# Reordering the last output tiles of a six-layer cross network and sharing them among three engines, on one Trainium2 core

## The chip, the cores and the metric

The kernel runs on one core of one Trainium2 chip. The metric is device time in microseconds (us). A profile of one execution comes with each kernel; its span, from the first to the last instruction, is about 1.7 us shorter than the device time (128.2 us for 129.92 in the profiled run of the kernel before). Runs are compared in their fast state only.

## The reference

```python
# x0: 4096 x 416, ws: 6 x 416 x 416, bs: 6 x 416, all bf16
def reference(x0, ws, bs):
    x = x0
    for l in range(ws.shape[0]):
        x = x0 * (x @ ws[l] + bs[l]) + x
    return x
```

## The kernel before

The 4096 rows are worked in four groups of 1024. The 416 features are held transposed, as three chunks of 128 ("main") and 32 left over ("tail rows"). The last layer of the last group is done differently: TensorE produces eight output tiles of 128 rows in their natural orientation in PSUM, with the sums of earlier layers added by identity matmuls, and VectorE finishes each as (PSUM + 1) * x0. Then the tiles are stored. This end is all that the change touches.

TensorE's end:

```python
nat_tile(0); nat_tile(1)            # 3 matmuls each, 128x128 by 128x416
pe.wait_ge(s_q, NC)
nat_sums(0); nat_sums(1)            # 3 identity matmuls each
nat_tile(2); nat_sums(2)
# ... waits ...
for r in range(2):                  # the tail rows of all eight tiles, in two halves
    # ... r == 1 waits for VectorE's last layer result (s_xb, s_qD) ...
    for g in range(4):              # 32-row matmuls on four row tiles, into tile t = 2g + r
        pe.matmul(ps[:, NAT_BANKS[t], 0:D], lhsT=xt_sb[...], rhs=wl_sb[...], start=t >= 3, ...)
    for g in range(4):
        ins = pe.matmul(ps[:, NAT_BANKS[t], DF:D], lhsT=xot_sb[...], rhs=ident[...], start=False, ...)
ins.then_inc(s_nt, 3)               # tiles 0, 1 and 2 are complete
for t in range(3, JS):              # JS = 8
    nat_tile(t)
    nat_sums(t).then_inc(s_nt, 1)
```

VectorE's end and the stores (two tiles each, from the queues of SyncE and ScalarE in turn):

```python
for t in range(JS):
    dve.wait_ge(s_nt, max(t + 1, 3))
    dve.scalar_tensor_tensor(out=o_sb[:, j0 + t, :], in0=ps[:, NAT_BANKS[t], 0:D], scalar=1.0,
        in1=x0n_sb[:, t, :], op0=ALU.add, op1=ALU.mult).then_inc(s_o, 1)
# SyncE:
for j in (0, 4):
    sp.wait_ge(s_o, j + 2)
    sp.dma_start(out_v[:, j0 + j:j0 + j + 2, :], o_sb[:, j0 + j:j0 + j + 2, :]).then_inc(s_out, 16)
sp.wait_ge(s_out, 16 * (NS + 3))
# ScalarE: the same for j in (2, 6)
```

Of the kernel before, what the change touches and what calls it, by code (L numbers as in the profile page):

```python
# [7 lines left out]
ALU = mybir.AluOpType  # L8
# [3 lines left out]
def bass_standalone__dcn_v2_cross__recsys_kernel(  # L12
# [20 lines left out]
    with ExitStack() as es:  # L33
# [15 lines left out]
        t32_sb = sb("t32_sb", [128, 2, G], FP32)  # L49
        x0n_sb = sb("x0n_sb", [128, JS, D])  # L50
        wl_sb = sb("wl_sb", [128, D])
        xo_sb = sb("xo_sb", [128, NS, NC, SB])
        xot_sb = sb("xot_sb", [128, NS, G])
        ot_sb = sb("ot_sb", [128, NS, 2, 128])
# [26 lines left out]
        s_x0n, s_wl, s_nt = sem("s_x0n"), sem("s_wl"), sem("s_nt")  # L81
        s_ta, s_xt, s_sw = sem("s_ta"), sem("s_xt"), sem("s_sw")
        s_oT, s_ot, s_otc = sem("s_oT"), sem("s_ot"), sem("s_otc")
        s_out, s_o = sem("s_out"), sem("s_o")

        x0_v = x0.rearrange("(j p) d -> p j d", p=128)
        out_v = out.rearrange("(j p) d -> p j d", p=128)
# [19 lines left out]
            return ps[HALVES[h], 6 + h, 0:G]  # L107

        j0 = (NS - 1) * JS

        def load_wt(eng, g, a, b, done):
            n0, n1 = ((0, 256), (256, DF))[g % 2]
# [4 lines left out]
        @block.sync  # L117
        def _(sp):
            def load_rows(s):
                sp.dma_start_transpose(  # L120
                    x4_sb[:, s - 1:s, :], x0[s * SB:(s + 1) * SB, D - 128:D]
                ).then_inc(s_x4[s - 1], 16)
                sp.dma_start_transpose(
                    x0T_sb[:, :, s * SB:(s + 1) * SB], x0[s * SB:(s + 1) * SB, 0:DF]
                ).then_inc(s_x0T[s], 16)

            sp.dma_start(bsa_sb[1:L + 1, :], bs[:, :]).then_inc(s_bs, 16)
            sp.dma_start(xin_sb[:, 0:2, :], x0_v[:, 0:2, :]).then_inc(s_xin[0], 16)
            sp.dma_start(xin_sb[:, 4:6, :], x0_v[:, 4:6, :]).then_inc(s_xin[2], 16)
            sp.dma_start_transpose(x0T_sb[:, :, 768:SB], x0[768:SB, 0:DF]).then_inc(s_x0T[0], 16)  # L130
            for l in range(1, L):
                if l > 1:
                    sp.wait_ge(s_ti, (1, 2, 2, 2)[l - 2])
                if l == L - 1:
                    load_rows(1)
                sp.dma_start(w_sb[:, l, :, :], wmain(l)).then_inc(s_w[l], 16)
                if l == 1:
                    for g in range(4):
                        load_wt(sp, g, 1, L, s_wt[1])
            for s in range(NS - 1):  # L140
                n = (s + 1) * L
                sp.wait_ge(s_xa, NC * n)
                sp.wait_ge(s_xb, NC * n)
                for c in range(NC):
                    sp.dma_start_transpose(
                        o_sb[:, s * JS:(s + 1) * JS, c * 128:(c + 1) * 128], xo_sb[:, s, c, :]
                    ).then_inc(s_oT, 16)
                sp.wait_ge(s_xt, n)
                sp.dma_start_transpose(ot_sb[:, s, :, :], xot_sb[:, s, :]).then_inc(s_ot, 16)
                if s < NS - 2:  # L150
                    load_rows(s + 2)
                if s == 0:
                    for g in range(4):
                        sp.dma_start(wl_sb[lane(g), :], ws[L - 1, DF:D, :]).then_inc(s_wl, 16)
                if s == 1:
                    sp.dma_start(x0n_sb[:, :, :], x0_v[:, (NS - 1) * JS:NS * JS, :]).then_inc(s_x0n, 16)
                sp.wait_ge(s_oT, 16 * NC * (s + 1))
                sp.wait_ge(s_otc, s + 1)
                sp.dma_start(
                    out_v[:, s * JS:(s + 1) * JS, :], o_sb[:, s * JS:(s + 1) * JS, :]  # L160
                ).then_inc(s_out, 16)
            for j in (0, 4):
                sp.wait_ge(s_o, j + 2)
                sp.dma_start(
                    out_v[:, j0 + j:j0 + j + 2, :], o_sb[:, j0 + j:j0 + j + 2, :]
                ).then_inc(s_out, 16)
            sp.wait_ge(s_out, 16 * (NS + 3))

        @block.gpsimd
        def _(pool):  # L170
            pool.memset(ones_sb[:, :], 1.0).then_inc(s_ones, 1)
            def load_wc(i, g):
                a, b = ((0, 1), (1, L))[i]
                pool.dma_start(
                    wc_sb[lane(g), a:b, 32 * g:32 * g + 32], ws[a:b, DF:D, DF:D].rearrange("l p n -> p l n")
                ).then_inc(s_wc[i], 16)

            pool.wait_ge(s_ones, 1)
            pool.affine_select(
                out=ident[:, :], in_=ones_sb[:, 0:128], pattern=[[-1, 128]],  # L180
                compare_op=ALU.is_equal, fill=0.0, base=0, channel_multiplier=1,
            ).then_inc(s_set, 1)
            pool.affine_select(
                out=u_sb[:, :], in_=ones_sb[0:L + 1, 0:L], pattern=[[1, L]],
                compare_op=ALU.is_ge, fill=0.0, base=1, channel_multiplier=-1,
            ).then_inc(s_set, 1)
            for g in (0, 2):
                load_wt(pool, g, 0, 1, s_wtp)
            pool.wait_ge(s_zero, 1)
            for i in range(2):  # L190
                for g in (1, 3):
                    load_wc(i, g)

            for s in range(NS):
                pool.wait_ge(s_te, s + 1)
                for l in range(L):
                    n = s * L + l + 1
                    if n == NL:
                        break
                    if n == 1:  # L200
                        pool.tensor_scalar(
                            out=cq_sb[:, 0:NC + 1], in0=cb_sb[:, :, L - 1], scalar1=-1.0, scalar2=None, op0=ALU.add
                        ).then_inc(s_cq, 1)
                        pool.wait_ge(s_cq, 1)
                        pool.tensor_tensor(
                            out=cq_sb[:, NC + 1:NC + 2], in0=cq_sb[:, NC:NC + 1], in1=cb_sb[:, NC, L - 2:L - 1], op=ALU.subtract
                        ).then_inc(s_cq, 1)
                    pool.wait_ge(s_ta, n)
                    dst = xot_sb[:, s, :] if l == L - 1 else xt_sb[:, (l + 1) % 2, 0:G]
                    pool.tensor_tensor(  # L210
                        out=dst, in0=t32_sb[:, n % 2, :], in1=x0t_sb[:, s, 0:G], op=ALU.mult
                    ).then_inc(s_xt, 1)
                    if n == NL - 1:
                        pool.tensor_scalar(
                            out=xot_sb[:, s, :], in0=t32_sb[:, n % 2, :], scalar1=cq_sb[:, NC + 1:NC + 2], scalar2=None, op0=ALU.add
                        ).then_inc(s_qt, 1)
                    if l == 2 and s > 0:
                        pool.wait_ge(s_ot, 16 * s)
                        pool.tensor_copy(
                            out=o_sb[:, (s - 1) * JS:s * JS, DF:D].rearrange("p (g r) f -> p r g f", r=2),  # L220
                            in_=ot_sb[:, s - 1, :, :].rearrange("p r (g f) -> p r g f", f=DR),
                        ).then_inc(s_otc, 1)

        @block.tensor
        def _(pe):
# [172 lines left out]
            def nat_tile(t):  # L398
                rows = slice(t * 128, t * 128 + 128)
                for k in range(NC):  # L400
                    if k == 0 and t < 3:
                        pe.wait_ge(s_xa, NC * (NL - 1))
                        pe.wait_ge(s_q, t + 1)
                    pe.matmul(  # L404
                        ps[:, NAT_BANKS[t], 0:D], lhsT=xT_sb[:, (L - 1) % 2, k, rows], rhs=w_sb[:, L - 1, k, :],
                        start=t < 3 and k == 0, stop=True, skip_group_check=True,
                    )

            def nat_sums(t):
# [10 lines left out]
            pe.wait_ge(s_q, NC)  # L420
            nat_sums(0)
            nat_sums(1)
            nat_tile(2)
            nat_sums(2)
            pe.wait_ge(s_xt, NL - 1)
            pe.wait_ge(s_qt, 1)
            pe.wait_ge(s_wl, 64)
            for r in range(2):
# [4 lines left out]
                for g in range(4):  # L433
                    t, rows = 2 * g + r, slice(r * 128, r * 128 + 128)
                    pe.matmul(  # L435
                        ps[:, NAT_BANKS[t], 0:D], lhsT=xt_sb[lane(g), (L - 1) % 2, rows], rhs=wl_sb[lane(g), :],
                        start=t >= 3, stop=True, skip_group_check=True, tile_position=(32 * g, 0),
                    )
                for g in range(4):
                    t, rows = 2 * g + r, slice(r * 128, r * 128 + 128)  # L440
# [1 line left out]
                        ps[:, NAT_BANKS[t], DF:D], lhsT=xot_sb[lane(g), NS - 1, rows], rhs=ident[lane(g), lane(g)],  # L442
                        start=False, stop=True, skip_group_check=True, tile_position=(32 * g, 0),
                    )
            ins.then_inc(s_nt, 3)
            for t in range(3, JS):
                nat_tile(t)
                nat_sums(t).then_inc(s_nt, 1)

        @block.vector  # L450
        def _(dve):
# [41 lines left out]
            ).then_inc(s_qD, 1)  # L493
            dve.wait_ge(s_x0n, 16)
            for t in range(JS):
                dve.wait_ge(s_nt, max(t + 1, 3))  # L496
                dve.scalar_tensor_tensor(  # L497
                    out=o_sb[:, j0 + t, :], in0=ps[:, NAT_BANKS[t], 0:D], scalar=1.0,
                    in1=x0n_sb[:, t, :], op0=ALU.add, op1=ALU.mult,
# [3 lines left out]
        def _(act):  # L503
# [26 lines left out]
            for s in range(NS):  # L530
                for l in range(L):
# [27 lines left out]
                    if l >= 3 and s < NS - 1:  # L559
# [7 lines left out]
                            )  # L567
                        if l == L - 1:
                            ins.then_inc(s_te, 1)
            for j in (2, 6):  # L570
                act.wait_ge(s_o, j + 2)
                act.dma_start(
                    out_v[:, j0 + j:j0 + j + 2, :], o_sb[:, j0 + j:j0 + j + 2, :]
                ).then_inc(s_out, 16)


# [26 lines left out]
```

## Time and profile before

| what | value | where it is read |
|---|---|---|
| time | 129.84 us, median of 3 | runs |
| span | 128.2 us | page |
| first row-tile matmul of layer one | 8.25 us | timeline, below |
| first final VectorE tile, last one's end | 121.60, 125.68 us | timeline |
| last store: issue to landing | 2.1 us | DMA issues |

In the code the first layer waits for the input loads, and its start depends on them. It is read in the timeline as the first matmul of the 32-row form (columns: start, duration, engine, line, operation, tiles and shapes):

```profile
8.25 0.37 PE L358 MATMUL ps<-x0t_sb,wt_sb 32*128 32x512 bf16 x1
```

What lies between this moment and the end of the span, 128.18 - 8.25 = 119.93 us, I call **the count**. By the page, 90% of the chain that ended last is TensorE and 6% VectorE, and the count is what the change can alter, and it separates the change from the loads.

### The profile page before, as it was taken

The page shows a single profiled execution, that of the slowest core. Times are in us where ns is not written, and L with a number is a line of the kernel's source. Part 1 is how long each engine was busy: PE and PEld are TensorE (multiplying, and loading weights), DVE is VectorE, ACT ScalarE, POOL GpSimd, SP SyncE. Part 2 cuts the span into 40 slices and gives each one's busy share as a digit, 9 for nine tenths or more (in the row PEclk, how much of TensorE's full clock was granted, in tenths as well). Part 3 has the DMA queues.
Part 4 walks back from the last instruction along what each step waited for, and adds up shares of the span by engine and source line. Part 5 has one row for each costly group of instructions (what it writes and reads, how often), then busy time and mean ns, then how long its engine had stood idle before and what let it go on. Part 6 is the DMA issues. An engine that isn't in the chain of part 4 may idle for free.

```text
span 128.2 us, 5183 instructions
## 1 busy us (share of the span) xinstructions
PE 124.0 (97%) x2338; PEld 62.3 (49%) x2338; DVE 100.7 (79%) x156; ACT 68.9 (54%) x156; POOL 22.2 (17%) x42
## 2 busy tenths in 40 slices
PE   7999999999999999999999999999999999999990
PEld 5654444445444445445445445445445445444560
DVE  2349779779779779779779789788788798797792
ACT  0637357377736456476745555575754564567500
POOL 7512202102102103012012023022022023020400
PEclk9999999999999999999999999999999999999999
DMA  3973399500009699810008699940008900700025
GB/s 98 287 187 100 81 213 204 139 5 0 5 5 158 121 113 227 248 42 5 0 5 161 115 145 232 353 134 0 5 0 91 181 5 0 250 21 5 0 98 168
DMA packets 33601, 13.48 MB, mean 105 GB/s; under 512 B 24871, under 2 KB 33581, under 8 KB 33581
## 3 DMA queue, kind: packets, MB, share of 16 engines
q1 hardware_dynamic: 31804, 12.12, 45.9%
q10 hardware_dynamic: 1584, 0.99, 2.8%
q8 instruction: 18, 0.29, 1.0%
q0 software_dynamic: 192, 0.06, 0.2%
q14 instruction: 3, 0.02, 0.1%
HBM read 3.86 MB, written 3.41 MB: 57 GB/s over the span
## 4 chain that ended last, share of the span: by engine, by line
PE 90%; DVE 6%; ACT 1%; DVEq 0%; issue 0%; ACTq 0%
PE ps L227 79%; PE ps L358 10%; DVE o_sb L497 3%; DVE xT_sb L486 3%; PE ps L277 1%; ACT xo_sb L520 1%; DVE xo_sb L491 1%; DVEq L33 0%; PE ps L435 0%; PE ps L374 0%; PE ps L441 0%; DVEq L496 0%; ACTq L537 0%
## 5 line engine op out<-in xcount | busy, mean ns | idle before, releaser
L486 DVE SCALAR_TENSOR_TENSOR xT_sb<-ps,cb_sb,x0T_sb 128x512 bf16<-128x512 f32 x120 | 81.0, 745 | 16.5 <-PE ps L358 16.5
L227 PE MATMUL ps<-xT_sb,w_sb 128*32 128x512 bf16 (+1 forms) x1596 | 84.2, 364 | 0.0
L227 PEld LDWEIGHTS ps<-xT_sb,w_sb 128*32 128x32 bf16 x1596 | 40.9, 97 | 37.2 <-issue 4.0
L516 ACT ACTIVATE xt_sb<-xt_sb 32x256 bf16<-32x256 bf16 x76 | 31.5, 414 | 15.8 <-POOL xt_sb L210 15.1
L545 ACT ACTIVATE t_sb<-ps,cb_sb 64x256 f32<-64x256 f32 x46 | 21.6, 469 | 28.7 <-PE ps L227 28.4
L210 POOL TENSOR_TENSOR xt_sb<-t_sb,x0t_sb 128x256 bf16<-128x256 f32 x20 | 13.5, 674 | 81.5 <-ACT t_sb L545 81.5
L227 PE MATMUL ps<-x0T_sb,w_sb 128*32 128x512 bf16 (+1 forms) x336 | 18.8, 369 | 0.1
L486 DVE SCALAR_TENSOR_TENSOR xo_sb<-ps,cb_sb,x0T_sb 128x512 bf16<-128x512 f32 x18 | 12.1, 743 | 2.5 <-PE ps L358 2.5
L227 PEld LDWEIGHTS ps<-x0T_sb,w_sb 128*32 128x32 bf16 x336 | 8.7, 98 | 7.9 <-issue 1.3
L358 PE MATMUL ps<-xt_sb,wt_sb 32*128 32x512 bf16 x76 | 11.5, 379 | 0.0
L564 ACT ACTIVATE x0t_sb<-x_sb 32x256 bf16<-32x256 bf16 x24 | 9.9, 413 | 0.4
L374 PE MATMUL ps<-xt_sb,wt_sb 32*128 32x512 bf16 x38 | 7.4, 385 | 0.0
L358 PE MATMUL ps<-xt_sb,wc_sb 32*128 32x256 bf16 x76 | 7.3, 268 | 0.0
L358 PEld LDWEIGHTS ps<-xt_sb,wt_sb 32*128 32x128 bf16 x76 | 2.2, 92 | 8.1 <-DVE xT_sb L486 8.1
L404 PE MATMUL ps<-w_sb,xT_sb 128*128 128x416 bf16 x24 | 5.4, 340 | 0.0
L358 PEld LDWEIGHTS ps<-xt_sb,wc_sb 32*128 32x128 bf16 x76 | 3.8, 93 | 2.2
L497 DVE SCALAR_TENSOR_TENSOR o_sb<-ps,x0n_sb 128x416 bf16<-128x416 f32 x8 | 4.1, 582 | 0.7 <-PE ps L441 0.7
L210 POOL TENSOR_TENSOR xot_sb<-t_sb,x0t_sb 128x256 bf16<-128x256 f32 x3 | 2.0, 673 | 12.6 <-ACT t_sb L545 12.6
L520 ACT ACTIVATE xo_sb<-ps,cq_sb 128x512 bf16<-128x512 f32 x5 | 3.3, 686 | 1.1 <-PE ps L358 1.1
L227 PE MATMUL ps<-const-bfloat16-1.0 128*32 128x256 bf16 x44 | 2.7, 416 | 0.8 <-PEq L588 0.8
L511 ACT ACT_TABLE_LOAD x1 | 1.3, 1283 | 3.6 <-issue 3.6
L404 PEld LDWEIGHTS ps<-w_sb,xT_sb 128*128 128x128 bf16 x24 | 2.0, 98 | 1.4 <-DVE xT_sb L486 0.4
(44 smaller groups left out, 34.4 us busy)
## 6 DMA issues: line engine op xcount, KB each, us to landing
out_dram<-o_sb SPq DMA_DIRECT2D x3, 832.0 KB, 4.9
w_sb<-in_ws_dram SPq DMA_DIRECT2D x5, 312.0 KB, 4.4
x0n_sb<-in_x_dram SPq DMA_DIRECT2D x1, 832.0 KB, 5.6
xin_sb<-in_x_dram SPq DMA_DIRECT2D x2, 208.0 KB, 3.4
out_dram<-o_sb SPq DMA_DIRECT2D x2, 208.0 KB, 2.0
out_dram<-o_sb ACTq DMA_DIRECT2D x2, 208.0 KB, 2.1
w_sb<-in_ws_dram ACTq DMA_DIRECT2D x1, 312.0 KB, 3.7
xin_sb<-in_x_dram ACTq DMA_DIRECT2D x1, 208.0 KB, 2.6
```

The lines of the kernel that those rows point to most:

```text
L210: pool.tensor_tensor(out=dst, in0=t32_sb[:, n % 2, :], in1=x0t_sb[:, s, 0:G], op=ALU.mult).then_inc(s_xt, 1)
L227: return pe.matmul(dst, lhsT=lhsT, rhs=rhs, start=start, stop=True, skip_group_check=True, tile_position=(0, 32 * q),)
L358: return pe.matmul(dst, lhsT=lhsT, rhs=srct[lane(g), cols], start=l == 0 and start, stop=True, skip_group_check=True, tile_position=(32 * ...
L374: pe.matmul(ps[:, NC * h + 2, :], lhsT=wt_sb[lane(g), l, 0:128], rhs=srct[lane(g), :].rearrange("p (b r) -> p b r", b=2)[:, ::-1, :], star ...
L404: pe.matmul(ps[:, NAT_BANKS[t], 0:D], lhsT=xT_sb[:, (L - 1) % 2, k, rows], rhs=w_sb[:, L - 1, k, :], start=t < 3 and k == 0, stop=True, sk ...
L486: dve.scalar_tensor_tensor(out=dst, in0=ps[:, NC * half + c, :], scalar=cb_sb[:, c, l:l + 1], in1=x0T_sb[:, c, o:o + H], op0=ALU.add, op1= ...
L497: dve.scalar_tensor_tensor(out=o_sb[:, j0 + t, :], in0=ps[:, NAT_BANKS[t], 0:D], scalar=1.0, in1=x0n_sb[:, t, :], op0=ALU.add, op1=ALU.mul ...
L511: act.activation(out=x0T_sb[:, 1, h * 256:(h + 1) * 256], in_=psT[:, IN_BANKS[h][1], 0:256], func=ACTF.Copy).then_inc(s_inA, 1)
L516: ins = act.activation(out=buf[lane(g), G:2 * G], in_=buf[lane(g ^ 1), 0:G], func=ACTF.Copy)
L520: act.activation(out=xo_sb[:, NS - 1, c, half * H:(half + 1) * H], in_=ps[:, NC * half + c, :], func=ACTF.Identity, bias=cq_sb[:, c:c + 1] ...
L545: ins = act.activation(out=t32_sb[HALVES[h], n % 2, :], in_=tail(h), func=ACTF.Identity, bias=cb_sb[HALVES[h], NC, l:l + 1],)
L564: ins = act.activation(out=x0t_sb[lane(g), s + 1, swap * G:(swap + 1) * G], in_=x4_sb[96:128, s, r * G:(r + 1) * G], func=ACTF.Copy,)
```

## The change

Its intent: keep TensorE from waiting for VectorE inside the tail rows, take two of eight tiles off VectorE, and make the last store half as large. The core of the diff:

```diff
+            store(sp, 0, 2, 1, 1)          # tiles 0-1 after 1 VectorE and 1 GpSimd tile
+            store(sp, 2, 4, 2, 2)
+            store(sp, 7, 8, 6, 0)
+            sp.wait_ge(s_out, 16 * (NS + 4))
 ...
+            for i, t in enumerate(POOL_TILES):      # GpSimd, POOL_TILES = (1, 3)
+                pool.wait_ge(s_oA, i + 1)
+                pool.tensor_tensor(out=o_sb[:, j0 + t, :], in0=a32_sb[:, i, :], in1=x0n_sb[:, t, :],
+                    op=ALU.mult).then_inc(s_oP, 1)
 ...
-            nat_tile(2)
-            nat_sums(2)
+            for t in (2, 3):
+                nat_tile(t)
+                nat_sums(t)
 ...
-            ins.then_inc(s_nt, 3)
-            for t in range(3, JS):
+            ins.then_inc(s_nt, 4)
+            for t in range(4, JS):
 ...
             for t in range(JS):                     # VectorE
+                if t in POOL_TILES:
+                    continue
 ...
+            for i, t in enumerate(POOL_TILES):      # ScalarE
+                act.wait_ge(s_nt, 4)
+                act.activation(out=a32_sb[:, i, :], in_=ps[:, NAT_BANKS[t], 0:D],
+                    func=ACTF.Identity, bias=1.0).then_inc(s_oA, 1)
+            store(act, 4, 6, 4, 0)
+            store(act, 6, 7, 5, 0)
```

In the built programs SyncE has 56 instructions where it had 53, GpSimd 59 for 56, ScalarE 194 for 192, VectorE 162 for 164.

More of the change, by code (lines that the diff above doesn't have):

```diff
@@ L51, in bass_standalone__dcn_v2_cross__recsys_kernel @@
         wl_sb = sb("wl_sb", [128, D])
+        a32_sb = sb("a32_sb", [128, 2, D], FP32)
         xo_sb = sb("xo_sb", [128, NS, NC, SB])
@@ L83, in bass_standalone__dcn_v2_cross__recsys_kernel @@
         s_oT, s_ot, s_otc = sem("s_oT"), sem("s_ot"), sem("s_otc")
-        s_out, s_o = sem("s_out"), sem("s_o")
+        s_out, s_o, s_oP, s_oA = sem("s_out"), sem("s_o"), sem("s_oP"), sem("s_oA")
         x0_v = x0.rearrange("(j p) d -> p j d", p=128)
@@ L109, in bass_standalone__dcn_v2_cross__recsys_kernel, with store @@
         j0 = (NS - 1) * JS
+        POOL_TILES = (1, 3)
+        def store(eng, a, b, by_dve, by_pool):
+            eng.wait_ge(s_o, by_dve)
+            if by_pool:
+                eng.wait_ge(s_oP, by_pool)
+            eng.dma_start(out_v[:, j0 + a:j0 + b, :], o_sb[:, j0 + a:j0 + b, :]).then_inc(s_out, 16)
         def load_wt(eng, g, a, b, done):
@@ L161, in _ @@
                 ).then_inc(s_out, 16)
-            for j in (0, 4):
-                sp.wait_ge(s_o, j + 2)
-                sp.dma_start(
-                    out_v[:, j0 + j:j0 + j + 2, :], o_sb[:, j0 + j:j0 + j + 2, :]
-                ).then_inc(s_out, 16)
-            sp.wait_ge(s_out, 16 * (NS + 3))
+            store(sp, 0, 2, 1, 1)
+            store(sp, 2, 4, 2, 2)
+            store(sp, 7, 8, 6, 0)
+            sp.wait_ge(s_out, 16 * (NS + 4))
         @block.gpsimd
@@ L222, in _ @@
                         ).then_inc(s_otc, 1)
+            pool.wait_ge(s_x0n, 16)
+            for i, t in enumerate(POOL_TILES):
+                pool.wait_ge(s_oA, i + 1)
+                pool.tensor_tensor(
+                    out=o_sb[:, j0 + t, :], in0=a32_sb[:, i, :], in1=x0n_sb[:, t, :], op=ALU.mult
+                ).then_inc(s_oP, 1)
         @block.tensor
@@ L403, in nat_tile @@
                         pe.wait_ge(s_q, t + 1)
+                    if k == 0 and t == 3:
+                        pe.wait_ge(s_ta, NL - 1)
                     pe.matmul(
                         ps[:, NAT_BANKS[t], 0:D], lhsT=xT_sb[:, (L - 1) % 2, k, rows], rhs=w_sb[:, L - 1, k, :],
-                        start=t < 3 and k == 0, stop=True, skip_group_check=True,
+                        start=t < 4 and k == 0, stop=True, skip_group_check=True,
                     )
@@ L436, in _ @@
                         ps[:, NAT_BANKS[t], 0:D], lhsT=xt_sb[lane(g), (L - 1) % 2, rows], rhs=wl_sb[lane(g), :],
-                        start=t >= 3, stop=True, skip_group_check=True, tile_position=(32 * g, 0),
+                        start=t >= 4, stop=True, skip_group_check=True, tile_position=(32 * g, 0),
                     )
@@ L495, in _ @@
             for t in range(JS):
-                dve.wait_ge(s_nt, max(t + 1, 3))
+                if t in POOL_TILES:
+                    continue
+                dve.wait_ge(s_nt, max(t + 1, 4))
                 dve.scalar_tensor_tensor(
@@ L569, in _ @@
                             ins.then_inc(s_te, 1)
-            for j in (2, 6):
-                act.wait_ge(s_o, j + 2)
-                act.dma_start(
-                    out_v[:, j0 + j:j0 + j + 2, :], o_sb[:, j0 + j:j0 + j + 2, :]
-                ).then_inc(s_out, 16)
+            for i, t in enumerate(POOL_TILES):
+                act.wait_ge(s_nt, 4)
+                act.activation(
+                    out=a32_sb[:, i, :], in_=ps[:, NAT_BANKS[t], 0:D], func=ACTF.Identity, bias=1.0
+                ).then_inc(s_oA, 1)
+            store(act, 4, 6, 4, 0)
+            store(act, 6, 7, 5, 0)
 _INS = ['x0', 'ws', 'bs']
```

## The prediction

> **What bounds the kernel now.** I first read the page of the kernel before (share per engine), then its chain of waits, then the timeline of the last ten microseconds, then short windows with the transfer rate. A change at the end of the program can only be read from the end. The page says 97% TensorE, and the chain agrees up to 116 us: blocks of 84 matmuls back to back, which the change doesn't touch. From there the chain leaves TensorE:
>
> ```profile
> 116.17 0.70 ACT xo_sb L520
> ...
> 116.89 3.39 DVE xT_sb L486 x5
> 120.28 0.67 DVE xo_sb L491
> 120.95 0.14 issue
> 121.08 0.35 PE ps L435 x2
> ...
> 121.60 3.58 DVE o_sb L497 x7
> ```
>
> Columns: start, duration, what. VectorE's last layer operations end at 120.95, TensorE adds the second half of the "tail rows" (L435, L441), and VectorE then finishes eight output tiles. The timeline shows how near TensorE is to it:
>
> ```profile
> 120.29 0.33 PE L412 MATMUL ps<-ident,xo_sb 128*128 128x128 bf16 x3
> 120.55 0.35 PE L435 MATMUL ps<-wl_sb,xt_sb 32*128 32x416 bf16 x4
> ...
> 121.08 0.36 PE L435 MATMUL ps<-wl_sb,xt_sb 32*128 32x416 bf16 x4 [0.16 <-DVE xo_sb L491]
> ...
> 121.60 4.08 DVE L497 SCALAR_TENSOR_TENSOR o_sb<-ps,x0n_sb 128x416 bf16<-128x416 f32 x8 [0.66 <-PE ps L441]
> ...
> 122.71 2.37 SPq L164 DMA_DIRECT2D out_dram<-o_sb  x2
> ...
> 123.72 2.40 ACTq L572 DMA_DIRECT2D out_dram<-o_sb  x2
> ...
> 124.71 0.33 PE L412 MATMUL ps<-ident,xo_sb 128*128 128x128 bf16 x3
> ```
>
> TensorE stands idle 0.16 us inside the tail matmuls, and its last matmul ends at 124.71+0.33 = 125.04. VectorE's eight tiles take 4.08 us, the first starting at 121.60; with 0.58 for the last, the pitch is (4.08-0.58)/7 = 0.50, the last runs 125.09 to 125.68. So VectorE and TensorE reach the last tile within 0.05 us of one another: **two chains are tied**. After the compute, 2.5 of the 128.2 us are left for the last store. Windows of 0.2 us there (last two columns: share of the 16 DMA engines, GB/s):
>
> ```profile
> 126.40:126.60 0.20, 0.00 (x0) 0.00 (x0) 0.00 (x0) 0.00 (x0) 0.00 (x0) 1.00 0.00 0
> 126.60:126.80 0.20, 0.00 (x0) 0.00 (x0) 0.00 (x0) 0.00 (x0) 0.00 (x0) 1.00 0.65 225
> 126.80:127.00 0.20, 0.00 (x0) 0.00 (x0) 0.00 (x0) 0.00 (x0) 0.00 (x0) 1.00 1.07 366
> 127.00:127.20 0.20, 0.00 (x0) 0.00 (x0) 0.00 (x0) 0.00 (x0) 0.00 (x0) 1.00 1.04 354
> 127.20:127.40 0.20, 0.00 (x0) 0.00 (x0) 0.00 (x0) 0.00 (x0) 0.00 (x0) 1.00 0.39 121
> 127.40:127.60 0.20, 0.00 (x0) 0.00 (x0) 0.00 (x0) 0.00 (x0) 0.00 (x0) 1.00 0.00 0
> ```
>
> The last store is issued at 125.71, its data move from about 126.66 to 127.27 (0.61 us for 208 KB, the engines full), it lands 2.1 us after issue (127.8), and the end follows 0.4 us later. So a store costs about **0.95 us before the first byte, its bytes at some 350 GB/s, 0.55 us after the last byte**. The first store is issued at 122.71; its data begin at 123.6, and between the four stores the engines rest 0.3 us or so each.
>
> [...] The trace has 597 ns (512 columns) and 377 ns (256 columns) for copies out of PSUM, a slope of 0.86[...]. [...] The final operation reads PSUM and one SBUF tile. No run so far has GpSimd beside it; GpSimd's product beside the like-formed layer operation takes a steady 0.67 us.
>
> **Part 1: tail rows one tile later.** Tile 3's six matmuls, pitch 0.70 us (starts of L404 122.09, 122.79, 123.48, 124.18), move in front of the tail. First tail half: 120.55+0.70 = 121.25. By then VectorE's last layer result (120.95) is there, so the second half follows without the 0.16 us of idle: about 0.25 us after the first, 121.50, where it was 0.53 after. TensorE then starts tile 4 at 121.81 (0.31 after the second half, as before: 121.08 to 121.39). Before, tile 4 started at 122.09. **TensorE gains 0.28 us.** Its last matmul ends at 124.76. The price: the signal that frees tiles 0 to 3 comes with the tail, and the first VectorE start moves from 121.60 to about 122.03 (121.50 plus the 0.52 from second half to VectorE, 121.08 to 121.60). **The finishing starts 0.43 later.** The new wait on ScalarE's read of the tail bank was fulfilled at 118.42; it costs nothing.
>
> **Part 2: two tiles to ScalarE and GpSimd.** VectorE loses 2 x 0.50 = 1.0 us. Its tiles are 0 (122.03), 2 (122.53), 4 (123.03), 5 (123.53), 6 and 7. A tile can start about 0.95 us after its first matmul on TensorE (0.53+0.33 to its last matmul's end, 0.1 for the signal). Tile 5 is there at 121.81+0.70+0.95 = 123.46, tile 6 at 124.16, tile 7 at 124.86. So VectorE now waits for TensorE from tile 6, and the last tile ends at 124.86+0.58 = **125.44, which is 0.24 before 125.68**. [...] No engine is late for the end, but GpSimd is late for the **stores**.
>
> **Part 3: the stores.** Issue times, from the above: tiles 0-1 SyncE 123.76 (before 122.71), tiles 4-5 ScalarE 124.13, tile 6 ScalarE 124.76, tiles 2-3 SyncE 124.78 (before 123.72), tile 7 SyncE 125.46. SyncE needs 0.37 us for an issue, so tiles 2-3 free it at 125.15, in time. Alone, the one-tile store would have its data 0.95 after issue, at 126.41, take 0.3 and end at 126.71, a gain of 0.56 over 127.27. But it isn't alone. The five stores are 8 x 128 x 832 B = 852 KB, at 350 GB/s 2.43 us, and the first data can't flow before 123.76+0.93 = 124.69. Packed without a gap, and the issue times leave none (two stores in by 125.1, four by 125.75), the data end at 124.69+2.43 = **127.12**. That is later than 126.71, so the packed transfers set the end: gain 127.27-127.12 = 0.15 us. I round to 0.2, as the rate in full windows (up to 366) is a little above 350.
>
> **Sum.** Of 0.24 us from the compute and 0.3 from the shorter last store, most is eaten by stores that begin 1.05 us later and meet: -0.2 us. 129.84-0.2 = **129.65 us**.
>
> **The rivals.** *A: the stores don't collide* (two queues together run faster than one, or GpSimd is quicker). Then the whole 0.55 us appears: 129.3. For it: the loads near the start show windows of up to 393 GB/s with several queues. Against: 350 to 366 at a share of 1.0 in the store[...]. *B: GpSimd is slower than estimated*, at 1.3 us a tile: the first store goes at 124.04, tiles 2-3 at 125.34, SyncE is then busy until 125.71 and tile 7 waits behind it. Data end at 124.97+2.43 = 127.40: +0.13, so 129.95. For it: spans on GpSimd are rough, one of its operations (L214) took 928 ns for 256 columns. Against: 23 products at a steady 0.67. *C: VectorE stays the bound*, if the GpSimd operation holds up its reads: two blocked tiles would put back up to 0.5 us; about 130.0. [...] *D: the tail gains nothing*[...]: TensorE's 0.28 shrinks to 0.1, but packed stores hide that; 129.7.
>
> **Range and chances.** All rivals lie between 129.3 and 130.0, and the three runs before spread from 129.80 to 130.34. I take 129.25 to 130.05. Two per cent is 2.6 us, more than the whole last store, and nothing here can save or cost it: faster 0.01, within 0.98, slower 0.01.
>
> **What would show it.** Right: no TensorE wait on L491 inside the tail; first final VectorE operation near 122.0 and last ending near 125.4; GpSimd products near 1.0 us; DMA share near 1.0 without a rest from about 124.7 to 127.1; the SyncE wait for the stores ending near 127.6. Wrong: a rest of the DMA engines ahead of the last store (rival A, the end then at issue plus 1.8), GpSimd above 1.2 us (B), final VectorE operations longer than 0.6 us (C), or tile 4's first matmul after 121.9 (D).

The two durations that stand alone in the paragraph cut short (597 and 377 ns) are ScalarE's, and the 0.67 us there is GpSimd's for 128x256. Two terms of the forecast's sum: it took 0.61 us for a tile on ScalarE and 1.02 on GpSimd, by which GpSimd's two tiles end at 123.74 and 124.76 and their stores are issued at 123.76 and 124.78. With these terms the sum came to -0.2 us and 129.65. The changed kernel's trace has 0.515 and 0.977 us for them. It also shows what the forecast only assumed of the stores: in three windows in which both queues move rows (125.4 to 125.6, 126.0 to 126.2 and 126.6 to 126.8 us) the rate is 321, 358 and 341 GB/s, no more than the 366 that one store alone reached before.

## The result, and the profile after

The changed kernel took **130.44 us** (median of 6, 130.11 to 130.85) against 129.82 for the kernel before (6 runs, 129.74 to 130.34). The ratio is 1.0042, with an interval of 1.0018 to 1.0067. Ratios here are the mean time of one kernel's fast runs over that of the other's of the same rounds, so not quite the ratio of the medians. By the 2% rule it is "same", as predicted, but it lies outside the predicted range and on the other side of the kernel before.

The chain of waits of the changed kernel ends like this (start, duration, what; "issue" is time for which the profile shows no wait):

```profile
122.15 0.63 PE ps L419 x3
...
124.87 0.18 PE ps L427 x3
125.05 0.02 issue
125.07 0.59 DVE o_sb L515
```

TensorE now leads to the very last VectorE tile. VectorE's long piece on the chain is gone, which is what parts 1 and 2 were for. The timeline shows the start of the first layer, and the end (in brackets: how long the engine stood idle before, and what ended that):

```profile
8.59 0.38 PE L371 MATMUL ps<-x0t_sb,wt_sb 32*128 32x512 bf16 x1
...
121.58 0.35 PE L451 MATMUL ps<-wl_sb,xt_sb 32*128 32x416 bf16 x4
121.79 0.34 PE L451 MATMUL ps<-wl_sb,xt_sb 32*128 32x416 bf16 x4
122.22 0.93 ACT L590 ACTIVATE a_sb<-ps 128x416 f32<-128x416 f32 x2 [1.55 <-PE ps L457]
122.30 3.37 DVE L515 SCALAR_TENSOR_TENSOR o_sb<-ps,x0n_sb 128x416 bf16<-128x416 f32 x6 [1.03 <-PE ps L457]
122.88 1.91 POOL L233 TENSOR_TENSOR o_sb<-a_sb,x0n_sb 128x416 bf16<-128x416 f32 x2 [2.47 <-ACT a_sb L590]
```

Two things are to be seen. The first layer begins **0.34 us later** than in the profile before, so every later time is moved by that much. And the tail's halves follow one another (121.58, 121.79) without a wait: part 1 works. Less the 0.34, the first final VectorE tile starts at 121.96 and the last ends at 125.66 - 0.34 = 125.32.

The count is 128.79 - 8.59 = **120.20**, that is 0.27 above the kernel before, where the prediction had -0.2. The last stores show why. DMA issues of the changed kernel from o_sb (KB, us from issue to landing), of the final 1024 rows:

```profile
out_dram<-o_sb SPq DMA_DIRECT2D x2, 208.0 KB, 2.3
...
out_dram<-o_sb ACTq DMA_DIRECT2D x1, 104.0 KB, 2.7
out_dram<-o_sb SPq DMA_DIRECT2D x1, 104.0 KB, 2.7
```

Half the bytes take longer to land, 2.7 us, where the last 208 KB took 2.1 before:

```profile
out_dram<-o_sb ACTq DMA_DIRECT2D x2, 208.0 KB, 2.1
```

Windows at the end (no engine computes any more, so their columns are zero; the last two are the share of the 16 DMA engines and GB/s):

```profile
127.00:127.20 0.20, 0.00 (x0) 0.00 (x0) 0.00 (x0) 0.00 (x0) 0.00 (x0) 1.00 1.18 391
127.20:127.40 0.20, 0.00 (x0) 0.00 (x0) 0.00 (x0) 0.00 (x0) 0.00 (x0) 1.00 0.61 200
127.40:127.60 0.20, 0.00 (x0) 0.00 (x0) 0.00 (x0) 0.00 (x0) 0.00 (x0) 1.00 0.04 13
127.60:127.80 0.20, 0.00 (x0) 0.00 (x0) 0.00 (x0) 0.00 (x0) 0.00 (x0) 1.00 0.08 17
127.80:128.00 0.20, 0.00 (x0) 0.00 (x0) 0.00 (x0) 0.00 (x0) 0.00 (x0) 1.00 0.01 4
```

The transfers are nearly over at 127.4, and then a trickle goes on to 127.9. It is (13 + 17 + 4) GB/s x 0.2 us = 6.8 KB, about eight rows of 832 bytes. That is a sixteenth of the last store's 128 rows, and of the 16 increments of the semaphore at its landing 15 are in by 127.92 us and the last comes at 128.39. So I infer that **one DMA engine of the 16 does its whole share after the others are done** (the packet records name a queue, not an engine): all other rows end by 127.44 us, and eight follow one another from 127.50 to 127.87. The view of the DMA queues in the window 127 to 128 us tells what else was there (packets, MB, share; q1 carries SyncE's transfers, q10 ScalarE's: from 123.5 to 128 us they move 0.53 and 0.32 MB in the changed kernel, where these engines issue 520 and 312 KB). First the kernel before, then the changed one:

```profile
q10 hardware_dynamic: 130, 0.09, 28.7%
```

```profile
q1 hardware_dynamic: 138, 0.10, 31.4%
q10 hardware_dynamic: 29, 0.02, 5.4%
q14 instruction: 1, 0.01, 1.9%
```

One packet of kind "instruction" (8192 bytes in the packet record) starts at 127.20 us and takes 0.31: it ends at 127.50, when the eight late rows begin. I call it a fetch, by the name of its kind; what it loads, no record says. Before, the corresponding packet comes at 129.18 us, when the program is over.

### The profile page after: what moved, and what is told of

It is laid out like the page before. It is cut to its first block, busy times and chain, and to the rows that moved or that the text cites. A ratio compares the mean times of both kernels' runs of the same rounds, so it can differ in the third digit from the quotient of the medians.

```text
span 128.8 us, 5189 instructions
## 1 busy us (share of the span) xinstructions
PE 124.2 (96%) x2338; PEld 62.3 (48%) x2338; DVE 99.9 (78%) x154; ACT 69.8 (54%) x158; POOL 24.1 (19%) x44
## 4 chain that ended last, share of the span: by engine, by line
PE 96%; DVE 0%; issue 0%
PE ps L240 81%; PE ps L371 10%; PE ps L419 3%; PE ps L290 1%; PE ps L427 1%; DVE o_sb L515 0%; PE ps L451 0%; PE ps L387 0%; PE ps L457 0%
## 5 line engine op out<-in xcount | busy, mean ns | idle before, releaser
L240 PE MATMUL ps<-x0T_sb,w_sb 128*32 128x512 bf16 (+1 forms) x336 | 19.3, 375 | 0.0
L515 DVE SCALAR_TENSOR_TENSOR o_sb<-ps,x0n_sb 128x416 bf16<-128x416 f32 x6 | 3.3, 586 | 1.1 <-PE ps L457 1.0
```

Source lines behind the costliest of these rows:

```text
L240: return pe.matmul(dst, lhsT=lhsT, rhs=rhs, start=start, stop=True, skip_group_check=True, tile_position=(0, 32 * q),)
```

## The experiments

Sixteen runs. The table has what each profile shows. "Late engine" is how far the last of the 16 increments of the stores' semaphore comes behind the one before it; "fetch" is the start of the last 8 KB instruction packet; "landing" is that of the last store.

| kernel | start | count | late engine | landing | fetch at | ratio to before (95%) |
|---|---|---|---|---|---|---|
| before (first profile) | 8.25 | 119.93 | 0.03 | 2.1 | 129.18 | 1 |
| before_again | 8.21 | 119.94 | 0.04 | 2.1 | 129.14 | 1.0009 (0.9981 to 1.0038) |
| changed (first profile) | 8.59 | 120.20 | 0.47 | 2.7 | 127.20 | 1.0042 (1.0018 to 1.0067) |
| after_again | 7.81 | 120.22 | 0.51 | 2.7 | 126.45 | 1.0006 (0.9993 to 1.0019) |
| after_third | 8.08 | 120.20 | 0.49 | 2.7 | 126.69 | 1.0020 (0.9989 to 1.0051) |
| layout_only | 7.92 | 119.91 | 0.02 | 2.1 | 129.08 | 1.0004 (0.9987 to 1.0022) |
| four_stores | 7.89 | 119.74 | 0.02 | 2.2 | 126.62 | 1.0005 (0.9979 to 1.0031) |
| pool_2_3 | 8.41 | 120.11 | 0.49 | 2.6 | 126.93 | 1.0035 (1.0022 to 1.0048) |
| pad_sp | 8.09 | 120.22 | 0.48 | 2.7 | 126.71 | 1.0075 (0.9987 to 1.0162) |
| part1_only | 8.69 | 120.30 | 0.04 | 2.1 | 129.98 | 1.0043 (1.0008 to 1.0079) |
| part2_only | 8.05 | 119.91 | 0.04 | 2.1 | 127.08 | 1.0001 (0.9968 to 1.0033) |
| pad_act | 8.05 | 119.72 | 0.04 | 2.2 | 117.74 | 0.9983 (0.9959 to 1.0007) |
| pad_act_again | 7.85 | 119.73 | 0.04 | 2.2 | 117.84 | 1.0002 (0.9946 to 1.0058) |
| pool_2_3_pad_act | 9.79 | 119.60 | 0.04 | 2.1 | 119.76 | 0.9986 (0.9946 to 1.0026) |
| split_only | 8.65 | 119.54 | 0.03 | 1.7 | 129.18 | 0.9954 (0.9922 to 0.9986) |
| split_act2 | 8.51 | 119.53 | 0.00 | 1.7 | 127.18 | 0.9985 (0.9958 to 1.0012) |
| split_again | 8.27 | 119.54 | 0.04 | 1.7 | 128.84 | 0.9963 (0.9934 to 0.9991) |

Counts of one kernel agree within 0.02 us, while the starts scatter over 0.9 us and once reach 9.79. Times carry both. (The sixteenth run, pad_pool, has no row here, for its profile can't be used; pad_sp's wide interval comes from one run at 131.89.) So questions of the end are read from the counts, and times are used for what they can decide.

### Chance, layout, or the stores?

**after_again**: no edit. Theory P says that the late end belongs to the packed stores, L that the new tensor's place in memory delays the start, N that all of it is noise.

> The changed kernel once more, for a second profile. In its first profile the time over my prediction has two parts: the first layer starts late (the first L371 at 8.59 us where the kernel before has it at 8.25), and one DMA engine ends the last store late (packets trickle from 127.4 to 127.9 us, the store lands 2.7 us after issue where before it is 2.1). Theory P (packed stores): the late end of the last store belongs to the change and comes again, landing 2.4 us or more after issue; the late start is chance of the loads and is gone or differs, and the time is again 130.1 to 130.8 us. Rival L (layout): the late start belongs to the change, because the new 3.3 KB tensor moves all later tensors in memory, and comes again at 8.5 to 8.7 us. Rival N (noise): both are gone and the time is 129.7 us or less.

The late engine is there again (0.51 us, landing 2.7, an instruction packet at 126.45). The late start is not: 7.81 us. The count repeats, but the time is 129.79, no higher than before: in the profiled run this start, 0.44 us ahead of that in the first profile of before, more than hides the late end. So P's reading of the end holds, its forecast of the time doesn't, and N holds for the start alone.

**layout_only**: the kernel before with the new tensor.

```diff
         wl_sb = sb("wl_sb", [128, D])
+        a32_sb = sb("a32_sb", [128, 2, D], FP32)
```

> The kernel before with the new tensor a32_sb allocated and not used: memory layout alone. Theory P: 129.8 us, ratio 1.000 within 0.1%, the first layer at 8.2 to 8.3 us. Rival L: the first layer starts at 8.5 to 8.7 us and the time is 130.1 to 130.2 us, ratio 1.002 to 1.003.

Start 7.92, count 119.91: layout does nothing. L falls.

**four_stores**: the last store undivided.

```diff
-            store(sp, 7, 8, 6, 0)
 ...
-            store(act, 6, 7, 5, 0)
+            store(act, 6, 8, 6, 0)
```

> The changed kernel with the last 256 rows stored by one transfer again (ScalarE's queue), four stores in all. Theory P (the stores are packed because the first ones begin late, and the split is not the cause): bytes still move without rest from 124.5 to about 127.1, the end is that of the changed kernel within 0.3 us either way, 130.1 to 130.6 us. Rival S (the fifth transfer, by its issue and its queueing behind another on SyncE's queue, makes the late landing): the last store lands 2.1 us after issue and the time is 129.6 to 129.8 us.

The count falls to 119.74 and the late engine is gone. This spoke for rival S (the fifth, one-tile store), and against the packing as the cause of the lateness, for the bytes are as packed here. It left two suspects: the one-tile store itself, and the instruction packet, which here came at 126.62, when the last store had only 0.15 us to go.

**pool_2_3**: another pair of tiles for GpSimd.

```diff
-        POOL_TILES = (1, 3)
+        POOL_TILES = (2, 3)
 ...
-            store(sp, 0, 2, 1, 1)
+            store(sp, 0, 2, 2, 0)
```

> The changed kernel with ScalarE and GpSimd finishing tiles 2 and 3 in place of 1 and 3, so VectorE's first two results leave at 123.1 us in place of 123.8 to 123.9. Theory P: the engines of the DMA start 0.8 us earlier (near 124.05), rest a little between the first and second store, and are done before 127.0; landing of the last store goes to about 2.1 to 2.3 us after issue; time 129.4 to 129.8 us, 0.6 to 0.8 under the changed kernel. Rivals L and S: the last store's landing and the start stay as in the changed kernel, 130.1 to 130.6 us.

The first store leaves earlier, as meant, but the late engine costs 0.49 us again, and the count is 120.11. My expectation failed: the gap ahead of the stores doesn't keep the late engine away.

### Whose fetch is it?

Now the theory was F: the late packet is a load of instructions for one engine, and its moment depends on how many instructions that engine has run. It was a guess from the packet's kind, to be tested. The change lengthened the streams of SyncE, GpSimd and ScalarE. Eight instructions more on one of them should move its fetch to a much earlier moment, where no store is.

**pad_pool**:

```diff
+        pad_sb = sb("pad_sb", [128, 8])
 ...
             pool.wait_ge(s_ones, 1)
+            for i in range(8):
+                pool.memset(pad_sb[:, i:i + 1], 0.0)
```

> The changed kernel with eight one-column memsets added on GpSimd early in the program. In all three profiles with five stores so far, one 8 KB transfer of the kind that the profile calls instruction (queue 14) falls into the last store (127.20 us in the changed kernel's first profile), and the last eight packets of one DMA engine come after it, 0.45 us behind the other 15; before the change the same transfer comes at 129.2 us, after the end. To take out the chance of the loads I count from the first row-tile matmul of layer one to the span's end: before 119.93, changed kernel 120.20 and 120.22. Theory F (an instruction fetch, whose moment depends on how many instructions an engine has run, delays one DMA engine): if GpSimd is the one whose three added instructions brought it forward, eight more move it out of the last store to far earlier, the last store lands 2.1 to 2.2 us after issue and the count falls to 119.7 to 119.8. If GpSimd isn't the one, fetch and count stay (120.2). Rival S (the one-tile store is slow by itself): landing stays 2.7 us, count 120.2, wherever the fetch is.

Inconclusive. The profiled execution took 443 us: TensorE's layer matmuls took 1018 ns on average in it, in place of 364. An instruction packet was still 3 us ahead of that span's end, which speaks against GpSimd, but I rest nothing on such a run. The timed ones (131.01, 131.01, 130.35; ratio 1.0079, 1.0035 to 1.0124) have no profile, so why they are slower than the changed kernel's stays open.

**pad_sp**: sixteen satisfied waits in SyncE's code, which became eight instructions (64 for 56 in the built program).

```diff
                 if s == 0:
+                    for i in range(16):
+                        sp.wait_ge(s_bs, 16)
```

> The same with eight wait instructions added on SyncE (waits that were fulfilled long before) in place of GpSimd's. Theory F: if SyncE is the engine whose fetch it is, the queue-14 transfer moves to an earlier time, count from the first row-tile matmul 119.7 to 119.8, the last store lands 2.1 to 2.2 us after issue; if it is not, 120.2 and 2.7. Rival S: 2.7 us and 120.2 whatever the fetch does.

Nothing moved: packet at 126.71, late engine 0.48, count 120.22. It is not SyncE's.

**pad_act**: the same on ScalarE.

```diff
             act.wait_ge(s_cb, 1)
+            for i in range(16):
+                act.wait_ge(s_bs, 16)
```

> The changed kernel with eight wait instructions (fulfilled long before) added on ScalarE's stream before its layer loop. SyncE's eight moved nothing (queue-14 transfer still in the last store, straggler still there, count 120.22), GpSimd's eight left it near the end as well. Theory F, now with ScalarE as the engine, whose stream the change made two instructions longer: the transfer leaves the last store for 113 to 119 us (eight ScalarE instructions earlier), the 16 DMA engines end the last store within 0.2 us of one another, landing 2.1 to 2.3 us after issue, count from the first row-tile matmul to the end 119.7 to 119.8 (kernel before 119.93, changed kernel 120.20 to 120.22). Rival S (the one-tile store is slow by itself): landing 2.7, count 120.2.

All of theory F came. The packet moved to 117.74 us; the queue view of 117 to 119 us has it (queue 8 carries 16 KB packets of the kind "instruction" all through the program, 18 of them in the kernel before and in the changed one):

```profile
q8 instruction: 1, 0.02, 3.2%
q14 instruction: 1, 0.01, 1.5%
```

The five stores are issued at the same moments as in the changed kernel, within 0.003 us when counted from the first layer's start (the last at 117.107 there, 117.108 here), and the last lands 0.5 us sooner, with no trickle in the windows:

```profile
out_dram<-o_sb SPq DMA_DIRECT2D x1, 104.0 KB, 2.2
```

```profile
126.60:126.80 0.20, 0.00 (x0) 0.00 (x0) 0.00 (x0) 0.00 (x0) 0.00 (x0) 1.00 0.84 283
126.80:127.00 0.20, 0.00 (x0) 0.00 (x0) 0.00 (x0) 0.00 (x0) 0.00 (x0) 1.00 0.12 33
127.00:127.20 0.20, 0.00 (x0) 0.00 (x0) 0.00 (x0) 0.00 (x0) 0.00 (x0) 1.00 0.00 0
```

Count 119.72: eight instructions that do nothing take 0.48 us off the changed kernel. The fetch moves with ScalarE's instruction count (126.69 us in after_third, 117.74 here) and not with SyncE's (126.71 in pad_sp; the starts are 8.08, 8.05 and 8.09), so I put it down to ScalarE, and its collision is the cause. Its moment can be counted: in every profile here, pad_pool's too, this packet starts within 1.9 us after the end of ScalarE's 190th recorded instruction. In the kernel before, that is the closing one at 128.12 us, with the program over; in the changed kernel, two instructions longer, it is the issue of ScalarE's last store at 125.00; in pad_act an operation of the layer loop, at 117.28.

**split_act2**: split_only (below) with four waits, which became two instructions, on ScalarE, so 194 as in the changed kernel.

> The last run's kernel with two wait instructions more on ScalarE, the number that the change added there. Theory F: the instruction transfer comes in at 126.8 to 127.4 us, at or in the last store, and can hold one DMA engine: count up to 0.45 above split_only's. If it comes only after the data of the last store (near 127.0), the count is that of split_only within 0.1 and the transfer's time alone shows that it is ScalarE's. Rival S: both alike, and no transfer before the end.

The packet is at 127.18, where split_only has it at 129.18: two instructions on ScalarE bring it forward by 2 us, as the change did. It cost nothing (119.53 and 119.54), though it began 0.08 us before this kernel's last row was written (127.26); so did the packets of four_stores and part2_only, 0.15 and 0.08 us before theirs. So a fetch close to the last data was not enough: in these runs it cost something only where eight rows of the last store came after it, which I read as its engine's own. In all five profiles with a late engine the fetch began 0.23 to 0.25 us before the others were done, and the late engine's eight rows, all of them, begin when the fetch ends. They then take 0.31 to 0.37 us, for up to three of them last 0.05 to 0.09 us in place of 0.04; so the engine is later by more than the packet's 0.31 to 0.37. What stays open: the packet follows the end of ScalarE's last store issue after 1.7 to 1.8 us in these five, but after 1.2 to 1.3 in four_stores, part2_only and split_act2. No run here tells why.

### What each part is worth

**part1_only**: tail rows later, all tiles on VectorE, four stores.

```diff
-        POOL_TILES = (1, 3)
+        POOL_TILES = ()
 ...
-            store(sp, 0, 2, 1, 1)
-            store(sp, 2, 4, 2, 2)
-            store(sp, 7, 8, 6, 0)
+            store(sp, 0, 2, 2, 0)
+            store(sp, 4, 6, 6, 0)
 ...
-            store(act, 4, 6, 4, 0)
-            store(act, 6, 7, 5, 0)
+            store(act, 2, 4, 4, 0)
+            store(act, 6, 8, 8, 0)
```

> Tail rows one tile later alone: VectorE finishes all eight tiles, four stores as before. By the prediction's arithmetic VectorE starts 0.4 us later and has no tile less, so its last ends 0.4 us later than before, and each store leaves 0.4 later: count from the first row-tile matmul 120.3 (before 119.93), the last store landing 2.1 us after issue, no fetch inside it, time 130.1 to 130.3 us at an average start. If TensorE and not VectorE set the end, it would be 119.7.

120.30, as worked out: alone it costs 0.37. VectorE runs its eight tiles without a pause, only later:

```profile
122.40 4.08 DVE L513 SCALAR_TENSOR_TENSOR o_sb<-ps,x0n_sb 128x416 bf16<-128x416 f32 x8 [1.03 <-PE ps L455]
```

**part2_only**: four_stores with TensorE's order of before.

```diff
-            for t in (2, 3):
-                nat_tile(t)
-                nat_sums(t)
+            nat_tile(2)
+            nat_sums(2)
 ...
-            ins.then_inc(s_nt, 4)
-            for t in range(4, JS):
+            ins.then_inc(s_nt, 3)
+            for t in range(3, JS):
 ...
-                act.wait_ge(s_nt, 4)
+                act.wait_ge(s_nt, max(t + 1, 3))
```

> Tiles 1 and 3 by ScalarE and GpSimd alone: tail rows where they were, four stores of two tiles. TensorE then sets the last tile (its last matmul where it was before), VectorE waits for it: compute ends within 0.1 us of before; the first store leaves about 0.45 us earlier than in the changed kernel, but 0.6 later than before; the last two-tile store is issued as before and finds the engines nearly free: count from the first row-tile matmul 119.9 to 120.0. GpSimd has the three instructions more here too, so by theory F the queue-14 transfer falls near the end again; if it falls into the last store, up to 0.3 more.

119.91, no gain: VectorE, with two tiles less, stops for TensorE (the bracket), which is as late as before.

```profile
122.78 2.68 DVE L511 SCALAR_TENSOR_TENSOR o_sb<-ps,x0n_sb 128x416 bf16<-128x416 f32 x4 [0.30 <-PE ps L424]
```

**split_only**: the kernel before with its last store split.

```diff
 # ScalarE
-            for j in (2, 6):
-                act.wait_ge(s_o, j + 2)
-                act.dma_start(out_v[:, j0 + j:j0 + j + 2, :], ...)
+            for a, b in ((2, 4), (6, 7)):
+                act.wait_ge(s_o, b)
+                act.dma_start(out_v[:, j0 + a:j0 + b, :], ...)
 # SyncE
+            sp.wait_ge(s_o, JS)
+            sp.dma_start(out_v[:, NJ - 1:NJ, :], ...)
```

> The kernel before with its last store split into tile 6 (ScalarE's queue) and tile 7 (SyncE's) and nothing else; ScalarE's stream has as many instructions as before. Theory F: no instruction transfer in the last store, one-tile store lands 2.0 to 2.2 us after issue less 0.3 for half the bytes, count 119.55 to 119.7, the last DMA engine within 0.2 us of the others. Rival S: the one-tile store lands 2.5 to 2.7 us after issue as in the three five-store kernels, count 119.9 to 120.3.

This settles rival S: the one-tile store lands after 1.7 us when nothing is in its way.

```profile
out_dram<-o_sb ACTq DMA_DIRECT2D x1, 104.0 KB, 1.9
out_dram<-o_sb SPq DMA_DIRECT2D x1, 104.0 KB, 1.7
```

Count 119.54, 0.39 below the kernel before, ratio 0.9954. **The split alone is worth more than the whole change.**

**pool_2_3_pad_act**: pool_2_3 and pad_act together, as a candidate.

> A candidate to beat both: tiles 2 and 3 to ScalarE and GpSimd, so that the first two tiles leave 0.7 us earlier, and eight wait instructions on ScalarE against the fetch. Theory F: count 119.6 (that of the version without the waits, 120.11, less the 0.49 that its one late DMA engine cost), 0.3 below the kernel before; time 129.3 to 129.5 at an average start. Rival S: 120.1, no better than the kernel before.

119.60 as forecast, that is 0.51 under pool_2_3. Its profiled run happened to start at 9.79 us and took 131.13; the other five took 129.40 to 130.04. It is no better than split_only, which needs none of it.

### The start, and the versions side by side on one chip

**before_again**, no edit:

> The kernel before, submitted as a kernel, for the scatter of its own start. Theory C (the late start of the changed kernel's first profile was chance of the input loads): the first row-tile matmul starts anywhere between 7.8 and 8.7 us, as it did over all kernels so far; the count from there to the end is 119.93 within 0.03. Rival K (the start belongs to the kernel): it starts at 8.2 to 8.3 us again.

**after_third**, no edit:

> The changed kernel a third time. Theory C: start between 7.8 and 8.7 us, count 120.2 within 0.05 with the instruction transfer in the last store again; of the timed runs only that 0.27 is the kernel's, ratio 1.002. Rival K: start at 8.5 to 8.7 us, ratio 1.004 to 1.005.

**pad_act_again**, the edit of pad_act:

> The changed kernel with eight waits more on ScalarE, for times on the same chip as the changed kernel: count 119.72 within 0.05; timed 0.2 below the kernel before and 0.5 below the changed kernel (ratio 0.998). If the fetch were not what cost the 0.5 us, it would be timed like the changed kernel.

**split_again**, the edit of split_only:

> The kernel before with its last store split, on the same chip: count 119.54 within 0.05, timed 0.4 below the kernel before (ratio 0.997), the fastest of the four.

The changed kernel's start, here from the timelines of after_again and then of after_third, is not its own:

```profile
7.81 0.37 PE L371 MATMUL ps<-x0t_sb,wt_sb 32*128 32x512 bf16 x1
```

```profile
8.08 0.39 PE L371 MATMUL ps<-x0t_sb,wt_sb 32*128 32x512 bf16 x1
```

With 8.59 in its first profile the same program has started at three times, and split_only, with no more on TensorE than the kernel before, at 8.65 and 8.27. before_again's 8.21 would have fitted rival K (the start belongs to the kernel), but after_third's start doesn't. The counts came as forecast, all four within 0.01. The medians on this chip are 130.00 (before_again), 130.06 (after_third), 129.46 (pad_act_again, its five fast runs) and 129.44 (split_again). after_third's ratio is 1.0020, which is what 0.27 us makes of 129.8. pad_act_again's is 1.0002, with an interval of 0.6% to either side, because one run at 131.20 counts as fast; by its times alone it would be unclear, and its count (119.73) and its median carry it. split_again is faster than before outside its interval.

## Why the prediction was wrong

Its times of the engines and of the stores' issues came within 0.2 us, and the total for the stores' data too, though that one in part by luck. The predicted times, against the changed kernel's first profile less 0.34 us for the later start:

| step | predicted | measured less 0.34 |
|---|---|---|
| tile 4's first matmul | 121.81 | 121.74 |
| first final VectorE tile | 122.03 | 121.96 |
| ScalarE, GpSimd per tile | 0.61, 1.02 | 0.515, 0.977 (durations) |
| first store's issue (tiles 0-1) | 123.76 | 123.59 |
| last VectorE tile's end | 125.44 | 125.32 |
| last store's issue | 125.46 | 125.35 |
| end of the data, 15 engines | 127.12 | 127.10 |
| end of the data, 16th engine | 127.12 | 127.53 |

- **Part 1** was right: no wait inside the tail rows, and VectorE starting 0.4 us later. part1_only shows the price by itself (+0.37).
- **Part 2** was right too: by itself it gains nothing, for TensorE sets the end (part2_only), and with part 1 it does: the last tile ends at 125.32 where 125.44 was predicted, and four_stores has -0.19. Two terms were mis-sized, and the outcome did not turn on their error. ScalarE's tile: I took the operation of 512 columns with a bias from memory (686 ns; a copy of that size without it takes 597) for one with a constant bias. The measured 0.515 us is 0.09 less. GpSimd's tile: the rate per element behind the 1.02 us was tested against one size only, with the fixed part left free. The two sizes now in the trace, 673 ns for 256 and 977 for 416 elements, give 1.90 ns per element, and the measurement decides. Rival C did not come: VectorE's tiles took 580 to 592 ns beside GpSimd, 580 to 591 before.
- **Part 3** was right as far as "packed transfers set the end": rival A, a whole 0.55 us, did not appear, and pad_act, in which the packed stores are undisturbed, has the count 0.21 below before. That is the predicted -0.2, but its terms were off and happened to cancel. By the packet records of pad_act, put on the time scale of the kernel before, the data begin at 124.48 (predicted 124.69) and the 852 KB take 2.61 us, which is 326 GB/s (predicted 2.43 at 350). And I had misread the last store of before in windows of 0.2 us: its rows end at 127.39, not 127.27, so 0.40 us ahead of the landing and not 0.55. The data then ended 0.30 us sooner, not 0.15, and a landing 0.49 us behind its data took back 0.09. four_stores, with the split undone, is only 0.02 worse, so the split is hidden once the stores are packed. The split's own worth came out a little larger than the 0.3 that I gave it: 0.39 where nothing hides it.
- **The step that failed** is in part 3, "The five stores are 8 x 128 x 832 B = 852 KB, at 350 GB/s 2.43 us". It treats the 16 DMA engines as one pipe with nothing else in it. But the last store landed with its slowest engine (the 16th increment at 128.39 us, the 15th at 127.92), and that engine, as I read the records, had an 8 KB instruction fetch of ScalarE to carry, 0.24 us ahead of the end of the others' data and before any of its own eight rows. It cost 120.20 - 119.72 = 0.48 us, more than the gain. I had asked what each added instruction costs its engine, and not what it does to the engine's stream: two instructions on ScalarE moved that fetch from 129.2 us into the last store. None of my rivals A to D had this. D's sign, a late tile 4, did not come either.
- **The range** failed for that, and for a second reason: it took 129.84 as a firm base. With the count's +0.27 alone the median would have been about 130.1, just outside. The other 0.35 in the first timing fits its later start (0.34 in the profiled run) and went away in the next two sets of runs. That it is not the kernel's, the same program's starts at 7.81 and 8.08 show; what sets the start of a given run, beyond the input loads that it waits for, is open. The three runs of before with their 0.5 us of spread were a warning.
- "Within 2%", and the reason for it, that nothing at the end can cost 2.6 us, held.

## What to carry to other kernels

Before a small gain at the end of a program is judged, cut the span at a moment after the loads: here the count repeated within 0.02 us while the times scattered by 0.5. Here the last store was as late as the slowest of its DMA engines, 0.47 us behind the others, so look for what else is on them, instruction packets too: two instructions more on ScalarE moved one from 129.18 to 127.20 us, into the last store, and eight idle ones more, placed early, moved it out of the way, to 117.74. And try each part alone: here the split of the last store gave 0.39 us by itself, and the two other parts, by delaying the first stores and packing all of them, left it next to nothing.
